# An attention and feed-forward kernel: a fifth tile takes the second product by seven products, and the work around it is laid out again

## The chip, the cores and the metric

The kernel runs on one core of one Trainium2 chip. A core has five engines that run their own streams of instructions and wait for one another by semaphores: TensorE (PE in the profile; PEld is its loading of weights), VectorE (DVE), ScalarE (ACT), GpSimd (POOL) and SyncE (SP, which here issues every transfer). The metric is the device time of one execution in microseconds (us); the figure for a kernel is the median of its runs.

## The reference

Two parts follow each other. The first is a linear attention over 8 batches of 8 heads, with 576 positions and 64 features each; its result is normalised and laid side by side into x, 4608 rows of 512. The second is a feed-forward layer with 2048 inner features.

```python
kv = np.einsum('bhsd,bhse->bhde', k, v)
out = np.einsum('bhsd,bhde->bhse', q, kv)
rms = np.sqrt(np.mean(out * out, axis=-1, keepdims=True) + 1e-06)
attn = out / rms * g_norm
x = attn.transpose(0, 2, 1, 3).reshape(4608, 512)
h = x @ w_in                      # 512 -> 2048
g = h * (1.0 / (1.0 + np.exp(-h)))
return (g @ w_out).astype(np.float32)
```

q, k, v and g_norm are float32; w_in and w_out arrive as float64 and are turned into float32 pairs on the chip.

## The kernel before

**Numbers.** TensorE multiplies in a float32 form with fewer bits. So each operand is kept as an upper part (rounded to that form) and a lower part (what is left, also in that form), and a product is three multiplies: upper by lower, lower by upper, upper by upper. An upper part is made by a copy on ScalarE, a lower part by a subtraction on VectorE or GpSimd. The names `gh`/`gl` are such a pair for the gated values; `wi f` and `wo f` hold both parts of block f (of 16, `NF`) of w_in and w_out.

**Tiles.** The 4608 rows are 9 tiles of 512 (`NT`), run one after the other. A tile goes through 8 steps (`HF`), each of which makes two blocks of 128 inner features (f and f + 8) and gives them to the second product. There are three ways to do that. Tiles 0 and 1 multiply plainly. Tiles 2 to 4 use `pair_step`: the first product of a step, a 2 by 2 product of blocks, is made by seven block products instead of eight (`product`, L782: 7 x 6 = 42 multiplies of 128x256); the second product is plain (`project`, which calls `halves`, L556: 48 multiplies), and runs a step behind. Tiles 5 to 8, set by `OUT7 = 5`, use `seven_step`: here the second product too is made by seven (`multiply`, L958: 42 multiplies), for which sums of the gated values (`first_forms`, `last_form`, `lower_summed`, L917 to L931) and sums of blocks of w_out are needed. The results of a tile of sevens are put together at the end of the tile or within the next one (`copies`, `sums`, `after_switch`). The last tile ends in `seven_end`.

**Order.** The order of the instructions of every engine is that in which the program writes them. Besides the products there are jobs, kept in tables by step g (16 of them in a tile, so 2 in a pair step or a seven step) and by the place in the step (`first_jobs`, `mid_jobs`, `last_jobs`: thirds): the attention of batches 2 to 7 (`plan`), a batch being a block of 80 small multiplies (`mm_kv`, L278) and four groups (`mm_out`, L383) with two transposes, a scaling and a reduction on VectorE for each (L340, L348, L398, L402), with the inverse roots of the batch (L524, L529, L532, L250 to L252); the sums of blocks of w_in (`make_sums`, in tile 1, L636 to L645) and of w_out (`make_out_sums`, in tiles 2 to 4); the sums of x and the operands of the next tile (`sums_of_x`, L726, `make_lower`, L774); and loads. The sums of both weights begin with `whole`, which adds the two parts of a block to the full value (L636 for w_in, L668 for w_out), on VectorE. Sums of w_out go to DRAM as two stores of 512 KB for each j, and come back in tiles 5 to 8 with three or four loads of 256 KB in each step.

**Banks.** PSUM has 8 banks: four accumulate the second product (`acc`), two take the first (`hp`), two are left to attention and, from tile 5 on, to the sevens (`at`, `other`). VectorE adds what the products leave in `hp` (L836 to L864 in pair steps, L1169 to L1215 in sevens) and so frees the bank for the next step's products. In `seven_step` the second product is a queue of 42 multiplies a step that is taken in four windows, `W7 = 12, 11, 11, 8`, between the first product's multiplies.

## Time and profile before

| what | value |
| --- | --- |
| runs | 801.3, 812.69, 812.34 us; median 812.34 |
| profiled execution | span 810.6 us; it has no time of its own beside the span |
| PE busy | 799.9 us, 99% of the span, 7340 instructions |
| DVE busy | 593.1 us, 73%, 1280 instructions |
| ACT busy | 392.9 us, 48%, 817 instructions |
| POOL busy | 112.4 us, 14%, 116 instructions |
| DMA | 171.08 MB; queue 1 takes 61.4% of the sixteen engines' span |

Busy time is the time in which an instruction of the engine ran. Multiplies are pipelined, so a busy TensorE says only that it had work, not at which pace it went. The pace is read from a timeline: two rows that stand at the same place of two steps in a row, their starts, and the multiplies between. Of the windows below, 107.6 to 212 us is tile 1, 212 to 495 the tiles 2, 3 and 4 with the first step of tile 5 (which still finishes tile 4), and 574 to 653 a tile of sevens.

### The profile page before, as it was taken

The page shows a single profiled execution, that of the slowest core. Times are in us where ns is not written, and L with a number is a line of the kernel's source. Part 1 is how long each engine was busy: PE and PEld are TensorE (multiplying, and loading weights), DVE is VectorE, ACT ScalarE, POOL GpSimd, SP SyncE. Part 2 cuts the span into 40 slices and gives each one's busy share as a digit, 9 for nine tenths or more (in the row PEclk, how much of TensorE's full clock was granted, in tenths as well). Part 3 has the DMA queues.
Part 4 walks back from the last instruction along what each step waited for, and adds up shares of the span by engine and source line. Part 5 has one row for each costly group of instructions (what it writes and reads, how often), then busy time and mean ns, then how long its engine had stood idle before and what let it go on. Part 6 is the DMA issues. An engine that isn't in the chain of part 4 may idle for free.

```text
span 810.6 us, 18450 instructions
## 1 busy us (share of the span) xinstructions
PE 799.9 (99%) x7340; PEld 780.3 (96%) x7340; DVE 593.1 (73%) x1280; ACT 392.9 (48%) x817; POOL 112.4 (14%) x116
## 2 busy tenths in 40 slices
PE   8999999999999999999999999999999999999997
PEld 7899999999999999999999999999999999999997
DVE  4999955788667678666767577678867876787666
ACT  4887544434434445435534444336534543464343
POOL 2799771332000000000000000000000000000000
PEclk9999999999999999999999999999999999999999
DMA  9994013645466946866576338876676567657553
GB/s 347 412 410 131 1 60 116 210 164 207 172 217 219 312 150 226 297 230 236 175 253 217 130 131 278 277 242 210 212 246 206 192 203 254 198 183 235 183 182 118
DMA packets 86744, 171.08 MB, mean 211 GB/s; under 512 B 8322, under 2 KB 47746, under 8 KB 86658
## 3 DMA queue, kind: packets, MB, share of 16 engines
q1 hardware_dynamic: 86658, 169.90, 61.4%
q8 instruction: 58, 0.95, 0.5%
q14 instruction: 28, 0.23, 0.1%
HBM read 137.36 MB, written 32.51 MB: 210 GB/s over the span
## 4 chain that ended last, share of the span: by engine, by line
PE 91%; DMA 4%; POOL 2%; issue 1%; DVE 1%; SPq 1%; ACT 0%; DVEq 0%; POOLq 0%; ACTq 0%
PE hp L782 34%; PE acc L556 26%; PE acc L958 11%; PE hp L556 9%; PE at L958 5%; DMA wi<-in_moe_w_in 3%; PE hp L958 3%; PE at L278 2%; PE at L383 2%; DMA k<-in_k 1%; POOL wo L217 1%; SPq L267 0%; POOL gl L577 0%; DVE ob L1009 0%; POOL wo_full L183 0%
## 5 line engine op out<-in xcount | busy, mean ns | idle before, releaser
L556 PE MATMUL acc<-wo,gh 128*128 128x256 f32 x1280 | 201.1, 277 | 0.2 <-POOL wo L217 0.2
L556 PEld LDWEIGHTS acc<-wo,gh 128*128 128x128 f32 x1280 | 170.2, 188 | 4.0 <-issue 3.5
L782 PE MATMUL hp<-x_second,wi 128*128 128x256 f32 x1152 | 156.5, 280 | 0.0
L782 PEld LDWEIGHTS hp<-x_second,wi 128*128 128x128 f32 x1152 | 143.1, 188 | 4.1 <-issue 3.9
L556 PE MATMUL acc<-wo,gl 128*128 128x256 f32 x640 | 124.6, 276 | 0.0
L782 PE MATMUL hp<-operand,wi 128*128 128x256 f32 x912 | 122.8, 279 | 0.3 <-DVE wi L864 0.2
L782 PEld LDWEIGHTS hp<-operand,wi 128*128 128x128 f32 x912 | 113.1, 188 | 0.8 <-DVE wi L864 0.4
L556 PEld LDWEIGHTS acc<-wo,gl 128*128 128x128 f32 x640 | 96.4, 188 | 0.0
L904 ACT ACTIVATE wi<-wi 128x512 f32<-128x512 f32 x64 | 40.5, 632 | 102.3 <-DVE wi L1206 78.0
L1009 POOL TENSOR_TENSOR e<-e,partial 128x256 f32<-128x256 f32 x2 | 1.5, 732 | 606.6 <-DVE e L1009 606.6
L958 PE MATMUL acc<-wo,gh 128*128 128x256 f32 x256 | 48.1, 281 | 0.0
L556 PEld LDWEIGHTS hp<-x_second,wi 128*128 128x128 f32 x384 | 44.8, 188 | 3.1 <-issue 2.6
L556 PE MATMUL hp<-x_second,wi 128*128 128x256 f32 x384 | 47.1, 279 | 0.0
L556 PE MATMUL hp<-x,wi 128*128 128x256 f32 x360 | 44.5, 278 | 0.8 <-POOL x L507 0.8
L958 PE MATMUL acc<-s,gs 128*128 128x256 f32 x288 | 44.1, 281 | 0.0
L556 PEld LDWEIGHTS hp<-x,wi 128*128 128x128 f32 x360 | 42.4, 188 | 1.2 <-POOL x L507 1.0
L1206 DVE TENSOR_TENSOR wi<-hp,partial 128x256 f32<-128x256 f32 x32 | 13.6, 425 | 38.9 <-PE hp L782 38.9
L958 PEld LDWEIGHTS acc<-wo,gh 128*128 128x128 f32 x256 | 39.0, 188 | 0.0
L958 PEld LDWEIGHTS acc<-s,gs 128*128 128x128 f32 x288 | 38.3, 189 | 0.0
L782 PE MATMUL hp<-moved,wi 128*128 128x256 f32 x288 | 37.8, 281 | 0.0
L1191 ACT COPY wi<-hp 128x256 f32<-128x256 f32 x32 | 11.9, 372 | 52.0 <-PE hp L782 52.0
L958 PE MATMUL acc<-wo,gl 128*128 128x256 f32 x128 | 35.9, 281 | 0.0
(213 smaller groups left out, 1559.7 us busy)
## 6 DMA issues: line engine op xcount, KB each, us to landing
wi<-sums_in_dram SPq DMA_DIRECT2D x112, 512.0 KB, 3.5
s<-out_sums SPq DMA_DIRECT2D x96, 256.0 KB, 4.4
wi<-in_moe_w_in SPq DMA_DIRECT2D x16, 512.0 KB, 8.0
wo<-in_moe_w_out SPq DMA_DIRECT2D x16, 512.0 KB, 9.0
sums_in_dram<-sum_parts SPq DMA_DIRECT2D x16, 512.0 KB, 2.9
out_sums<-wi SPq DMA_DIRECT2D x16, 512.0 KB, 2.9
k<-in_k SPq DMA_DIRECT2D x28, 288.0 KB, 5.1
v<-in_v SPq DMA_DIRECT2D x28, 288.0 KB, 5.3
```

The source lines that it names most:

```text
L217: nc.gpsimd.tensor_tensor(out=w[:, 1, :], in0=full, in1=w[:, 0, :].bitcast(F32), op=ALU.subtract)
L278: nc.tensor.matmul(out=self.kv[h], lhsT=self.k[rows, c, :], rhs=self.v[rows, c, :], start=(start and r == 0), stop=(stop and r == 4),)
L383: nc.tensor.matmul(out=self.banks[r][to], lhsT=kv[rows, 2 * self.u + i], rhs=self.q[rows, i * HS:(i + 1) * HS], start=True, stop=True,)
L556: nc.tensor.matmul(out=to[:, at:at + 256], lhsT=stationary, rhs=moving[:, at:at + 256], start=start and at == 0, stop=stop and at == n - 256,)
L782: nc.tensor.matmul(out=out, lhsT=a_of(i, a, c), rhs=x[b][:, c], start=start and n == 0, stop=n == 5, skip_group_check=not check,)
L904: nc.scalar.activation(out=self.gated, in_=self.gated, func=AF.Silu)
L958: nc.tensor.matmul(out=self.out[m], lhsT=g[m], rhs=self.weight(m, j, a), start=j == 0 and n == 0 and m in self.opens, stop=j == HF - 1 and ...
L1009: engine.tensor_tensor(out=to, in0=x, in1=y, op=op)
L1191: nc.scalar.copy(out=first.gated[:, low], in_=u)
L1206: nc.vector.tensor_tensor(out=first.gated[:, high], in0=u, in1=u3, op=ALU.add)
```

## The change

`OUT7` becomes 4: tile 4 too takes the second product by seven, so tiles 2 and 3 alone are pair tiles. What hangs on it is moved. All of attention's multiplies are now done before tile 4 by new tables of thirds (`PLANS`, `QUARTERS`, `SUMS`, `OUT_SUMS`). The adds of `whole` go to GpSimd, all 32 of them. The w_out sums are stored in four parts of 256 KB for each j, straight from the tiles in which they are made. In `seven_step` the operations of the two halves are joined into one where they stood side by side; the queue takes products 1, 2, 3 of both halves and then 5, 7, 6, 4 of both, with `W7 = 11, 12, 11, 8`, and keeps 11 multiplies back from step to step (only the last step of the kernel empties it); the loads of w_out sums stand behind the first window. The first step of tile 4 (`opening`) finishes tile 3's second product by single multiplies, `OPENING = 10, 10, 9, 6`, and 13 more in the next step. Copies, sums and stores of a finished tile of sevens have a table of their own (`between`).

```diff
+QUARTERS = {
+    3: (133, 127, 119, 134),
+    4: (168, 166, 172, 178),
+}
+SUMS = (53, 58, 62, 63, 66, 71, 79, 82)
+OUT_SUMS = (99, 111, 117, 122, 128, 149, 159, 167)
+SUM_STAGES = (2, 4, 1, 1)
+OUT_STAGES = (0, 2, 3, 4, 6, 7)
...
+    OPENING = 10, 10, 9, 6
+    SECOND_AT = 3
     WARM = 2
-    OUT7 = 5
-    AT = {1: 3, 2: 14, 3: 23, 4: 32, 5: 41, 6: 51, 7: 60}
+    OUT7 = 4
...
+    places = const.tile([P, 6, TN], F32R, name="places")
+    gated_kvm = const.tile([P, 2, TN], F32, name="gated_kvm", tag="last_places")
...
+    def gated_place(n):
+        turns[n] += 1
+        return places[:, 3 * n + (turns[n] - 1) % 3]
...
+    def project_calls(t, f, gh, gl, bank, n, cs):
         first, last = order(t)[0], order(t)[-1]
         w = parts["wo", f]
         ns = slice(n * P, (n + 1) * P)
         bank = bank[:, :cs.stop - cs.start]
         terms = ((gh, 1), (gh, 0), (gl, 0)) if t else ((gh, 0), (gl, 0), (gh, 1))
-        for i, (g, a) in enumerate(terms):
-            halves(bank, g[:, ns], w[:, a, cs], f == first and i == 0, f == last and i == 2)
-        if f == last and t + 1 == OUT7:
-            emptied.append(lambda: empty(t, bank, n, cs, True))
-        elif f == last:
-            empty(t, bank, n, cs, n % 2)
+        columns = range(0, cs.stop - cs.start, 256)
+        def multiply(i, g, a, c):
+            nc.tensor.matmul(
+                out=bank[:, c:c + 256], lhsT=g[:, ns], rhs=w[:, a, cs][:, c:c + 256],
+                start=f == first and i == 0 and c == 0, stop=f == last and i == 2 and c == columns[-1],
+            )
+        def end():
+            if f == last and t + 1 == OUT7:
+                emptied.append(lambda: empty(t, bank, n, cs, True))
+            elif f == last:
+                empty(t, bank, n, cs, n % 2)
+        calls = [lambda i=i, g=g, a=a, c=c: multiply(i, g, a, c) for i, (g, a) in enumerate(terms) for c in columns]
+        return calls[:-1] + [lambda: (calls[-1](), end())]
+    def project(*item):
+        for call in project_calls(*item):
+            call()
...
+    def whole(engine, to, kind, f):
+        w = parts[kind, f].bitcast(F32)
+        engine.tensor_tensor(out=to, in0=w[:, 0, :], in1=w[:, 1, :], op=ALU.add)
...
-            lambda: whole(lower, i),
-            lambda: whole(upper, i + HF),
+            lambda: whole(nc.gpsimd, lower, "wi", i),
+            lambda: whole(nc.gpsimd, upper, "wi", i + HF),
...
-        def upper(two):
-            nc.scalar.copy(out=both_parts[:, 0], in_=two)
+        def upper(half, two):
+            nc.scalar.copy(out=uppers[:, half], in_=two)
         def lower(half, two):
-            nc.vector.tensor_tensor(out=both_parts[:, 1], in0=two, in1=both_parts[:, 0].bitcast(F32), op=ALU.subtract)
-            nc.sync.dma_start(out=out_sums[j, half], in_=both_parts.bitcast(F32))
+            nc.vector.tensor_tensor(out=two, in0=two, in1=uppers[:, half].bitcast(F32), op=ALU.subtract)
+            for part, w in enumerate((uppers[:, half].bitcast(F32), two)):
+                nc.sync.dma_start(out=out_sums[j, half][:, part], in_=w)
+        def first_three():
+            combine(s41[:, high], s41[:, high], s23[:, high], ALU.add)
+            combine(s23[:, high], s23[:, low], s23[:, high])
+            combine(s23[:, low], s41[:, high], s23[:, low])
+        def wholes():
+            whole(nc.gpsimd, s23, "wo", j)
+            whole(nc.gpsimd, s41, "wo", j + HF)
+        def fourth():
+            combine(s41[:, low], s41[:, low], s23[:, low])
+            upper(0, s23)
         return [
-            lambda: whole(s23, j),
-            lambda: whole(s41, j + HF),
-            lambda: combine(s41[:, high], s41[:, high], s23[:, high], ALU.add),
-            lambda: combine(s23[:, high], s23[:, low], s23[:, high]),
-            lambda: combine(s23[:, low], s41[:, high], s23[:, low]),
-            lambda: upper(s23),
-            lambda: combine(s41[:, low], s41[:, low], s23[:, low]),
+            wholes, first_three, fourth,
+            lambda: upper(1, s41),
             lambda: lower(0, s23),
-            lambda: None,
-            lambda: None,
-            lambda: None,
-            lambda: upper(s41),
-            lambda: None,
...
+    def both_lower_plain():
+        y = once["both_gated"]
+        nc.vector.tensor_tensor(
+            out=plain[1][:, :, :3 * P], in0=y[:, :, P:], in1=plain[0][:, :, :3 * P].bitcast(F32), op=ALU.subtract
+        )
+    def both_forms():
+        y, f = (once[name].rearrange("p h (k n) -> p h k n", n=P) for name in ("both_gated", "forms"))
+        nc.vector.tensor_tensor(
+            out=f[:, :, 0:2], in0=y[:, :, 1:3], in1=y[:, :, 0:1].to_broadcast([P, 2, 2, P]), op=ALU.subtract
+        )
+        nc.vector.tensor_tensor(out=f[:, :, 2], in0=y[:, :, 2], in1=f[:, :, 0], op=ALU.add)
+        nc.vector.tensor_tensor(out=f[:, :, 3], in0=y[:, :, 3], in1=f[:, :, 2], op=ALU.subtract)
+    def both_upper_summed():
+        nc.scalar.copy(out=summed[0], in_=once["forms"])
+    def both_lower_summed():
+        nc.vector.tensor_tensor(
+            out=summed[1], in0=once["forms"], in1=summed[0].bitcast(F32), op=ALU.subtract
+        )
     class Half:
...
-    W7 = 12, 11, 11, 8
+    W7 = 11, 12, 11, 8
...
-            (0, "I"): [c[0], *made_ahead(3)], (0, "II"): [c[1], c[2], a[0], a[1]], (0, "III"): a[2:4],
-            (1, ""): [lambda: nc.scalar.copy(out=fourths, in_=once["fourths"])],
-            (1, "I"): [d[0], d[1], *a[4:6]], (1, "II"): [d[2], a[6], b[0], b[1]], (1, "III"): b[2:4],
-            (2, "I"): b[4:6], (2, "II"): b[6:],
+            (0, ""): [*under(5), *uppers(3)], (0, "I"): under(3), (0, "II"): [c[0]],
+            (1, ""): [c[1], d[0], a[0]],
+            (1, "II"): [c[2], d[1], lambda: nc.scalar.copy(out=fourths, in_=once["fourths"]), d[2], a[1], a[2]],
+            (1, "III"): a[3:5], (2, ""): a[5:7], (2, "II"): [*b[0:2], a[7]], (2, "III"): [*b[2:4], a[8]],
+            (3, ""): b[4:6], (3, "II"): [b[6], b[7]], (3, "III"): b[8:],
         })
...
-            queue.extend(item for half in sevens for item in half.items(j, half.order))
+            for ms in (1, 2, 3), (5, 7, 6, 4):
+                queue.extend(item for half in sevens for item in half.items(j, ms))
         def window(n):
-            if opening:
-                for item in groups[:2]:
-                    project(*item)
-                del groups[:2]
+            if opening or ((t, i) == (OUT7, 1) and n == 0):
+                count = OPENING[n] if opening else len(groups)
+                for call in groups[:count]:
+                    call()
+                del groups[:count]
                 return
-            count = len(queue) if n == 3 else (W7 if later else (11, 10, 10))[n]
+            count = len(queue) if last and n == 3 else W7[n]
             for half, *item in queue[:count]:
...
-        load_out_sums(i, 5, 7, 6)
         begin(g)
         product(1, i, u, True, False)
         product(6, i, v, False, False)
         if not opening:
-            first.upper_summed()
-            second.upper_plain()
-            second.first_forms()
-            second.last_form()
-            first.lower_summed()
+            both_forms()
         nc.scalar.copy(out=p1, in_=u)
...
-        window(0)
+        if (t, i) != (OUT7, 1):
+            window(0)
+        load_out_sums(i, 5, 7, 6)
         if not opening:
-            second.lower_plain()
-            second.upper_summed()
-            second.lower_summed()
+            both_upper_summed()
...
+        if not opening:
+            both_lower_summed()
...
-        nc.vector.tensor_tensor(out=first.gated[:, high], in0=u, in1=u3, op=ALU.add)
-        nc.vector.tensor_tensor(out=second.gated[:, high], in0=v, in1=u3, op=ALU.add)
+        nc.vector.tensor_tensor(
+            out=once["both_gated"][:, :, high], in0=bank.rearrange("p (h n) -> p h n", n=H),
+            in1=u3.unsqueeze(1).to_broadcast([P, 2, H]), op=ALU.add,
+        )
         slot("III")
         first.gate()
         first.upper_plain()
-        first.first_forms()
+        if last:
+            first.first_forms()
         window(2)
         run(mid_jobs.pop(g + 1, ()))
         product(3, i, v, False, False)
         nc.vector.tensor_tensor(out=second.gated[:, low], in0=v, in1=u2, op=ALU.add)
         second.gate()
-        first.last_form()
-        first.lower_plain()
...
+        for n, (p, f) in enumerate(zip(ps, jobs)):
+            at_third(loads[n], lambda p=p: p.load(which="kv"))
+            at_third(q_loads[n], f.load)
+            at_third(jobs_at[n], lambda f=f: f.mm_out(kv[0]), f.copy_out)
+            at_third(turns[n], f.turn_sq)
+            at_third(sums_at[n], *[begin] * (n == 0), lambda f=f: f.sum_turned(norms[0]))
+            at_third(roots[n], lambda n=n: some((6, 3, 3, 3)[n]))
+            for part in (0, 1) if b == 2 else (None,):
+                at_third(scales[n], lambda p=p, part=part: p.spread(norms[1][:, p.c], part))
+                at_third(scales[n] + (b > 2), lambda p=p, part=part: p.scale(part))
+            at_third(keeps[n], p.keep)
+        at_third(kv_at, kv_block)
+        at_third(copy_at, copy_kv)
+        return ps
...
-        for j, g in enumerate((33, 37, 41, 49, 53, 57, 65, 69)):
-            spread_out(lambda j=j: make_out_sums(j), 3 * g, *[1] * 14)
+                at_third(QUARTERS[t][n], lambda t=t, n=n: load_quarter(t, n))
+        for j in range(HF):
+            calls = []
+            def some(j, calls=calls):
+                if not calls:
+                    calls.extend(make_out_sums(j))
+                calls.pop(0)()
+            for n in range(6):
...
```

Counted over the program, TensorE has 48 multiplies of 128x256 fewer (6885 to 6837) and all others as before; VectorE has 191 instructions fewer, ScalarE 18 fewer, GpSimd 32 more, and the transfer queue 42 more.

On TensorE, within tile 4, the order before has the plain second product (L556, `acc`) between the products of the first (L782, `hp`); `gh` and `gl` are the gated values.

```order
L556 MATMUL acc<-wo_583,gh 128x256 x4
L556 MATMUL acc<-wo_583,gl 128x256 x2
L782 MATMUL hp<-operand_3017,wi_564 128x256 x6
L782 MATMUL hp<-operand_3056,wi_3013 128x256 x6
L556 MATMUL acc<-wo_1408,gh 128x256 x4
L556 MATMUL acc<-wo_1408,gl 128x256 x2
```

The changed program has in the same tile, with `places` and `summed` in the place of `gh`, `gl` and `gs`, and `s` the sums of w_out (L889 is the first product, L1076 the second):

```order
L889 MATMUL hp<-x_second,wi_1134 128x256 x6
L889 MATMUL hp<-x_second,wi_2924 128x256 x6
L1076 MATMUL acc<-wo_1293,places 128x256 x3
L1076 MATMUL acc<-wo_574,places 128x256 x3
L1076 MATMUL at<-s,places 128x256 x2
L1076 MATMUL at<-s,summed 128x256
L1076 MATMUL hp<-s,places 128x256 x2
```

The second product of tile 4 now reads sums and writes the banks of attention (`at`, `hp`) as well.

On VectorE, a block of w_out sums in a pair tile before: `s_5668` and `s_5669` are the tiles in which the sums are made, L668 the adds of the two parts.

```order
L668 TENSOR_TENSOR s_5668<-wo_1059 128x512
L855 TENSOR_TENSOR gf<-hp,wi_3153 128x256
L856 TENSOR_TENSOR gf<-hp,wi_3153 128x256
L598 COPY wi_3249<-acc 128x512
L398 STREAM_TRANSPOSE sqT<-sq 128x576
L668 TENSOR_TENSOR s_5669<-wo_1774 128x512
L864 TENSOR_TENSOR wi_3153<-hp,wi_3153 128x256
L796 TENSOR_TENSOR gl<-gf,gh 128x512
```

In the changed program the two adds of such a block stand on GpSimd (L738), one behind the other:

```order
L738 TENSOR_TENSOR s_3834<-wo_765 128x512
L738 TENSOR_TENSOR s_3835<-wo_1439 128x512
```

and VectorE begins the block with the combinations (L774), the first of which waits for GpSimd:

```order
L774 TENSOR_TENSOR s_3835<-s_3835,s_3834 128x256 [waits Pool_49]
L774 TENSOR_TENSOR s_3834<-s_3834 128x256 [waits DVE_49]
L774 TENSOR_TENSOR s_3834<-s_3835,s_3834 128x256 [waits DVE_49]
L968 TENSOR_TENSOR wi_3084<-hp,wi_3084 128x256 [waits PE_49]
L903 TENSOR_TENSOR places<-gated_kvm,places 128x512 [waits Activation_49]
```

What frees a bank (L968, L864 before) stands behind the combinations and so behind GpSimd's adds.

On VectorE, the last pair step of tile 2 in the changed program, which makes the operands of the next tile (L881) and the sums of x (L833) beside attention's squares (L491, L495):

```order
L941 TENSOR_TENSOR wi_3084<-hp,wi_3084 128x256
L903 TENSOR_TENSOR places<-wi_3084,places 128x512
L833 TENSOR_TENSOR t_4149<-x_1_2037,t_4148 128x512
L491 STREAM_TRANSPOSE sqT<-sq 128x576
L951 TENSOR_TENSOR wi_3084<-hp,wi_3084 128x256
L881 TENSOR_TENSOR operand_2926<-x_0_1871,operand_2926 128x512
L881 TENSOR_TENSOR operand_2965<-t_4148,operand_2965 128x512
L495 TENSOR_REDUCE sums<-sqT 128x2x9
L960 TENSOR_TENSOR wi_3084<-hp,wi_3084 128x256
L961 TENSOR_TENSOR wi_3084<-hp,wi_3084 128x256
```

Before, that step held such operands with one transpose for attention; now it holds two transposes and two reductions.

## Rows read from the trace of the kernel before

**Rows 1.** The page: busy time, the granted clock in tenths, the chain.

```profile
PE 799.9 (99%) x7340; PEld 780.3 (96%) x7340; DVE 593.1 (73%) x1280; ACT 392.9 (48%) x817; POOL 112.4 (14%) x116
...
PEclk9999999999999999999999999999999999999999
...
PE 91%; DMA 4%; POOL 2%; issue 1%; DVE 1%; SPq 1%; ACT 0%; DVEq 0%; POOLq 0%; ACTq 0%
```

**Rows 2.** Windows: stretch, length; PE, PEld, DVE, ACT, POOL busy; clock, DMA.

```profile
107.60:212.00 104.40, 104.40 (x1036) 100.05 (x1037) 71.75 (x133) 45.39 (x97) 31.19 (x25) 1.00 0.47 168
212.00:495.00 283.00, 282.75 (x2718) 271.68 (x2717) 200.39 (x434) 125.78 (x267) 0.00 (x0) 1.00 0.63 211
574.00:653.00 79.00, 79.00 (x673) 79.00 (x673) 59.56 (x145) 38.79 (x78) 0.00 (x0) 1.00 0.66 213
```

**Rows 3.** Timeline of PE in tile 4: start, length, instruction.

```profile
472.89 1.52 PE L782 MATMUL hp<-operand,wi 128*128 128x256 f32 x12
...
483.09 1.52 PE L782 MATMUL hp<-operand,wi 128*128 128x256 f32 x12
```

**Rows 4.** The same view in tiles 5, 6 and 8.

```profile
503.12 1.73 PE L782 MATMUL hp<-operand,wi 128*128 128x256 f32 x12
...
592.32 1.58 PE L782 MATMUL hp<-moved,wi 128*128 128x256 f32 x12
...
602.21 1.58 PE L782 MATMUL hp<-moved,wi 128*128 128x256 f32 x12
...
795.48 1.56 PE L782 MATMUL hp<-moved,wi 128*128 128x256 f32 x12
...
801.00 0.40 PE L958 MATMUL hp<-s,gh 128*128 128x256 f32 x2
801.47 0.38 PE L958 MATMUL hp<-s,gl 128*128 128x256 f32 x1
```

**Rows 5.** The same view where attention stands in tile 2.

```profile
228.87 2.70 PE L278 MATMUL at<-v,k 128*64 128x64 f32 x80
...
251.80 0.39 PE L556 MATMUL acc<-wo,gl 128*128 128x256 f32 x2
252.12 0.72 PE L383 MATMUL at<-q,kv_all 64*64 64x288 f32 x8
252.77 1.64 PE L782 MATMUL hp<-x_second,wi 128*128 128x256 f32 x12
```

**Rows 6.** Groups on DVE, 215 to 495 us: busy, mean ns, idle before.

```profile
L796 DVE TENSOR_TENSOR gl<-wi,gh 128x512 fp32r<-128x512 f32 x24 | 16.4, 682 | 0.0
...
L348 DVE SCALAR_TENSOR_TENSOR o<-o,gcol,yT 128x576 f32<-128x576 f32 x18 | 14.6, 811 | 0.0
L340 DVE STREAM_TRANSPOSE yT<-y 128x576 f32<-128x576 f32 x18 | 13.9, 770 | 0.0
L398 DVE STREAM_TRANSPOSE sqT<-sq 128x576 f32<-128x576 f32 x18 | 13.8, 765 | 0.0
L402 DVE TENSOR_REDUCE sums<-sqT 128x18 f32<-128x576 f32 x18 | 13.4, 744 | 0.0
L668 DVE TENSOR_TENSOR s<-wo 128x512 f32<-128x512 f32 x16 | 10.8, 677 | 0.0
...
L836 DVE TENSOR_TENSOR wi<-hp,wi 128x256 f32<-128x256 f32 x24 | 10.2, 425 | 25.0 <-ACT wi L835 11.9 <-ACT kv_all L1297 7.2 <-PE hp L782 5.3
```

**Rows 7.** What PE waited for from 56 us on: total, times, longest.

```profile
PE hp L782 <- DVE wi L864: 0.2, 1, 0.2
```

**Rows 8.** Groups on POOL, and on DVE in 107 to 212 us.

```profile
L645 POOL TENSOR_TENSOR sum_parts<-sums,sum_parts 128x512 fp32r<-128x512 f32 x16 | 21.4, 1346 | 60.1 <-ACT sum_parts L644 60.1
...
L577 DVE TENSOR_TENSOR gl<-gf,gh 128x512 fp32r<-128x512 f32 x16 | 12.7, 792 | 26.5 <-ACT gf L576 23.5 <-issue 3.0
```

**Rows 9.** Timelines of POOL and DVE in tile 1.

```profile
179.48 2.54 POOL L645 TENSOR_TENSOR sum_parts<-sums,sum_parts 128x512 fp32r<-128x512 f32 x2 [6.84 <-ACT sum_parts L644]
...
180.94 1.64 DVE L577 TENSOR_TENSOR gl<-gf,gh 128x512 fp32r<-128x512 f32 x1 [1.90 <-ACT gf L576]
```

More of the change, by code (lines that the diff above doesn't have):

```diff
@@ L996, in sums @@
                 lambda: add(two[:, high], three[:, low], two[:, high], ALU.subtract),
-                upper_rows, lower_rows,
+                lambda: add(two[:, low], two[:, low], one[:, low]),
+                lambda: add(one[:, low], fourth(), three[:, low]),
+                lambda: self.store(t, 0, slice(0, DM), two),
+                store_lower,
             ]
@@ L1120, in seven_step @@
             open_sevens()
-        if (t, i) == (OUT7, 1):
-            first_banks()
-        first, second = sevens
+        last = (t, i) == (NT - 1, HF - 1)
+        if not opening:
+            first, second = sevens
         if t + 1 < NT and i == 5:
@@ L1173, in seven_step @@
             open_gated()
+            first, second = sevens
         while lowers:
@@ L1176, in seven_step @@
             make_lower(m, home(m))
+        if (t, i) == (OUT7, 1):
+            window(0)
+            second.upper_plain()
+        if not opening:
+            both_lower_plain()
         slot("")
@@ L1192, in seven_step @@
         nc.vector.tensor_tensor(out=u3, in0=v, in1=p1, op=ALU.add)
+        if not opening:
+            both_lower_summed()
         if later:
@@ L1216, in seven_step @@
         second.gate()
-        first.last_form()
-        first.lower_plain()
+        if last:
+            first.last_form()
+            first.lower_plain()
+        elif not opening:
+            second.upper_plain()
         if later:
@@ L1317, in plan, with some @@
-        for p in ps if b == 1 else ():
+        kv = []
+        loads, (kv_at, copy_at), q_loads, jobs_at, turns, sums_at, roots, scales, keeps = PLANS[b]
+        jobs = [Job(b, n, ps[n // 2 * 2:n // 2 * 2 + 2]) for n in range(NP)]
+        calls = []
+        def some(count):
+            if not calls:
+                calls.extend(rsqrt(*norms, False))
+            for _ in range(count):
+                calls.pop(0)()
[10 more added lines that the diff above has]
+            at_third(keeps[n], p.keep)
```

255 lines of the change are left out of this document (133 added, 122 removed).

## The prediction, as it was made before the changed kernel ran

> **What bounds the kernel now.** I read the page first: TensorE is busy for 99% of the span, VectorE for 73%, and 91% of the chain that ends last is TensorE [rows 1]. The reader is to see that no other engine or transfer sets the end over a longer stretch. The windows by tile say the same of each stage: from 107.6 us on TensorE is busy for the whole of each stretch, VectorE for 71% of the pair tiles and 75% of a tile of sevens, and the granted clock is 1.00, which is the 2.4 GHz level [rows 2]. The waits confirm it: from 56 us on only one wait is booked, 0.2 us for VectorE's L864 [rows 7]. So the time is the number of multiplies times their pace, and the next thing to read is the pace.
>
> In tile 4 two equal places of neighbouring steps lie 10.20 us apart (472.89 to 483.09) with 90 multiplies of 128x256 between: 113.3 ns each [rows 3]. In tile 6 the distance is 9.89 us (592.32 to 602.21) for 84: 117.8 ns [rows 4]. The pace changes at one place: the row at 503.12, the start of tile 5's third step, has twelve multiplies in 1.73 us where the row at 472.89 has 1.52; from there to about 796 us a row of twelve has 1.58, and at 795.48 it is on its way back to 1.52 [rows 3, 4]. The granted clock reads 1.00 on both sides. These 293 us hold about 29.6 steps of 84; at 4.44 ns each that is 11.05 us. The lowest run is 801.3, and 812.3 - 11.05 = 801.3. I take it that the profiled execution and the two runs at 812 have that stretch, and that the lowest run has not. What starts it the rows don't tell.
>
> The profiled execution has only its span, 810.6 us; the median of the runs is 812.34, 1.7 above. I make the sum against the span and add 1.7.
>
> **The change part by part.**
>
> *Fewer multiplies.* Tile 4 has 8 steps of 42 + 42 multiplies in place of 42 + 48: 48 fewer, none of another kind added. At 113.3 ns: 48 x 0.1133 = **-5.44 us**, all of it on the path, since TensorE is the path.
>
> *Pace of tile 4.* If the slower pace belongs to the sevens, it now begins a tile earlier: 8 x 84 x 4.44 ns = **+2.98 us**. If it doesn't, 0. It has its start in the sevens in the one execution that there is, so I take 2.98 and keep 0 as a rival.
>
> *Joined operations of the sevens.* VectorE does 59.56 us in a tile's 79 [rows 2], and no multiply of the sevens waits for it [rows 7]. Joining saves starts of instructions where nobody waits: 0. The queue's new order and the 11 multiplies held back give the next step's sums more time, and the loads of w_out sums behind the first window are used a step, some 9.9 us, later. Also 0. At the end of the kernel multiplies stand still for some tenths: the pair at 801.00 should be followed 0.24 later, and the next row starts at 801.47, 0.23 too late [rows 4]. There now stand 19 multiplies behind the last product where 11 stood, about 0.9 us more cover, for this and a second such gap: **-0.5**, bounds 0 and -0.5.
>
> *Opening and hand-over.* Tile 3's second product is finished by single multiplies in the opening and 13 in the second step: the same multiplies at the same pace, in another order. Result copies and stores go by another table; those of a tile of sevens lie beside multiplies, under VectorE's free quarter. 0, with 1 us either way for a bank that comes free late.
>
> *Transfers.* 32 stores of 256 KB in the place of 16 of 512, and 24 more loads of 256 KB (tile 4's) pass SP's queue, which is busy for 0.63 to 0.66 in these tiles [rows 2]. What hides them is the step between load and use. If that cover went, a load would cost its own time once, which the bound of 1 us above includes.
>
> *Pair tiles with more VectorE work each.* This is the part with a real price. Attention of six batches, the operands and all of the w_out sums must now be done before tile 4. In the 283 us of tiles 2 to 4 VectorE has 200.39 us of work [rows 2]. Of that go the own work of 8 steps (five operations like L836 at 0.425 and two like L796 at 0.682, 3.49 us a step, 27.9), and the sixteen adds of L668 (16 x 0.677 = 10.8) [rows 6]. Two of 18 attention groups (L348, L340, L398, L402: 3.09 us each, 6.2) stand in tile 1 now. That leaves about 156 us. TensorE in tiles 2 and 3 has 16 x 10.20 = 163.2, 16 groups of attention at about 0.86 (0.97 from 251.80 to 252.77, less two multiplies of 0.113, and 0.12 by which the twelve behind it are longer, 1.64 for 1.52) and three blocks of keys and values at some 2.6: about 185 [rows 3, 5]. So VectorE goes from 71% to 84%. Priced step by step with those rows, one step of sixteen has more work for VectorE than for TensorE: the last of tile 2, with five operations at 0.425, nine at 0.683, two transposes at 0.770 and two reductions at 0.744, 11.3 us, against 90 x 0.1133 + 0.86 = 11.1. Steps 4, 5 and 6 of that tile have some 0.8, 1.0 and 0.5 us to spare. The one wait of before, at L864, is such a step [rows 7].
>
> *GpSimd's adds.* An add of 128x512 on GpSimd takes 1.346 us (L645), on VectorE 0.677 [rows 6, 8]. GpSimd has nothing to do in the pair tiles (0.00 [rows 2]), so its own length costs nothing, but VectorE's first combination waits for the pair, and L864's successor, which frees TensorE's bank, stands behind that. And a running add lengthens what VectorE does beside it: the sixteen L577 have a mean of 0.792 where the like of L796 has 0.682, and one that began under two adds took 1.64 and ended at 182.58, 0.56 after the second add's end at 182.02 [rows 6, 8, 9]. It stood still for most of the add. Sixteen L577 lost 16 x 0.11 = 1.76 us, and in the timeline four of them are longer than 0.69: 0.44 each. Sixteen adds that each meet one such operation: 7 us, 0.9 for each of the eight blocks of sums, and a block's step has 0.5 to 4 us to spare. The excess is some tenths in two or three steps, with the full step of 11.3 beside them: **+1.0** in all. Bounds: 0, and 5.7 more under the rivals. In tile 1 the same happens under VectorE's 71.75 of 104.4 us [rows 2]: 0.
>
> The Trainium skill (SBUF — State Buffer, section "SBUF: two separate sides") has a rule that speaks against this part: VectorE with two inputs in SBUF and GpSimd share a port pair as a lock, and the one that comes second stands until the other's whole instruction is done. The row at 180.94 agrees with it; by the rule the adds would cost what the third rival below has, by the mean of L577 the 1.0 of the sum.
>
> **Sum.** -5.44 + 2.98 - 0.5 + 1.0 = -1.96; span 810.6 to 808.6, and with 1.7 for the median: **810.3 us**.
>
> **The rivals.** *First, the slower pace doesn't grow:* it starts by something else than the sevens, and lasts as long as before. For it: at 1.00 both stretches have the same granted clock. Against: it began two steps into the sevens, and the lowest run seems to lack all of it. Time: 810.3 - 2.98 = 807.4.
>
> *Second, no slower pace in the runs that make the median:* as the lowest run of before has it. 801.3 - 5.44 - 0.5 + 1.0 = 796.4. One of three runs speaks for it, two and the profiled one against.
>
> *Third, GpSimd's adds hold VectorE, and VectorE TensorE:* the place is the combination behind the two adds in the pair tiles. Two adds in a row take 2.54 us [rows 9]; if VectorE stands for both, a block costs 2.54 less what its step has to spare. With 1.0, 4.4, 0.8, 1.0, 0.5 in tile 2 and 2.7 or more in tile 3 (reckoned as above) that is 1.5 + 0 + 1.7 + 1.5 + 2.0 + 0 = 6.7, in place of the 1.0: 816.0, slower than before. It decides from 3.0 us on (5.44 - 2.98 + 0.5). For it: the long L577. Against: the adds of L577's stretch lengthened few of its operations, and five of the seven own operations of a step have an input in PSUM, as L836.
>
> *That the change does not do what it says* is excluded as far as the multiplies go: the 48 are gone from TensorE's order.
>
> **Chances.** Forecast 0.45; first rival 0.20, second 0.20, third 0.10; anything else (a late operand, a bank that comes free late, a load) 0.05. The range reaches from the second rival less 1 us of the unpriced parts to the third: 795.4 to 816.0. About 2% is what a measurement of this kernel can tell from no change; that is below 796.1 or above 828.6. Faster by more takes the lower half of the second rival: 0.10. Slower by more needs three times the third rival's price: 0.03. Same: 0.87.
>
> **What would show it.** In the profile after: 6837 multiplies of that kind; twelve multiplies in 1.52 in tiles 2 and 3 and 1.58 from tile 4's third step on (1.52 there: the first rival; 1.52 everywhere: the second). VectorE at about 84% of tiles 2 and 3; waits of TensorE for L968 there of some tenths, about 1 us in all (7: the third, with VectorE idle behind POOL, or operations such as L903 above 1 us). At the end no gap before the last sums. The forecast is wrong if tiles 2 and 3 take over 3 us more than their multiplies, or if the pace is another one.

## The result: slower by 1.4%, and the profile after

| | median | lowest to highest | runs |
| --- | --- | --- | --- |
| before | 802.24 us | 800.38 to 813.25 | 20 |
| changed | 814.61 us | 806.88 to 820.02 | 20 |

The changed kernel takes 1.0136 times as long, 95% interval [1.0108, 1.0164]. The time lies inside the range of the forecast and on its other side: 12.4 us longer instead of 2 shorter. The 812 us that stood as the median of before was that of three runs; of twenty, fifteen are at 800 to 803 and five at 812 to 813. So the slower pace, which the forecast took for the usual case, is before's exception.

The page of the changed kernel, profiled at a span of 808.9 us: busy time, the chain by line, one group of adds on GpSimd (mean 1514 ns), and the landing of two kinds of load.

```profile
span 808.9 us, 18271 instructions
...
PE 791.7 (98%) x7292; PEld 769.3 (95%) x7292; DVE 595.5 (74%) x1089; ACT 406.3 (50%) x799; POOL 158.5 (20%) x148
...
PE 60%; DMA 4%; DVE 4%; issue 0%; POOL 0%; DVEq 0%; SPq 0%; POOLq 0%
...
L738 POOL TENSOR_TENSOR s<-wo 128x512 f32<-128x512 f32 x16 | 24.1, 1514 | 136.8 <-DVE sqT L491 53.7
...
wi<-sums_in_dram SPq DMA_DIRECT2D x112, 512.0 KB, 4.4
s<-out_sums SPq DMA_DIRECT2D x120, 256.0 KB, 3.9
```

Against [rows 1], TensorE is idle for 17.2 us of the span (808.9 - 791.7) instead of 10.7. The chain is followed over 68% of the span only, so its 60% can't be set against 91%; but VectorE has 4% of it where it had 1%. The w_in sums land in 4.4 us where they took 3.5; the page of before has:

```profile
wi<-sums_in_dram SPq DMA_DIRECT2D x112, 512.0 KB, 3.5
```

What TensorE waited for in the changed kernel from 56 us on: total, times, longest. It answers to [rows 7].

```profile
PE hp L889 <- DMA wi<-sums_in_dram: 3.3, 3, 2.1
PE hp L889 <- DVE wi L941: 1.8, 1, 1.8
PE acc L703 <- DVE places L669: 0.5, 1, 0.5
PE hp L889 <- DVE partial L1285: 0.3, 1, 0.3
PE hp L889 <- DVE wi L1331: 0.2, 1, 0.2
PE hp L889 <- DVE wi L951: 0.2, 1, 0.2
PE hp L889 <- DVE wi L968: 0.2, 1, 0.2
```

The view leaves out what a pipelined engine loses around a wait. So for every profile I took the starts of the 128x256 multiplies from 56 us on. A distance over 121 ns counts as a standstill with what it has above 113.3 (the first one behind a group of attention is 221 or so in each profile without a wait, and counts with what it has above that); one of 115.5 to 121 counts as a multiply at the slower pace, with 4.44 ns.

| profile | span | standstills | slower pace | rest |
| --- | --- | --- | --- | --- |
| before | 810.6 | 1.9 | 11.4 | 797.3 |
| changed | 808.9 | 12.1 | 4.3 | 792.5 |

The rest fell by 4.8, near the 5.44 of the 48 multiplies. Standstills rose by 10.1, and that is more than the gain. Without any slower pace the changed kernel's row would give 792.5 + 12.1 and some 1.8 us from span to time, 806.4; the lowest of its twenty runs has 806.88. So most of its runs seem to have more of the slower pace than the profiled one; that is an estimate, since only one run has a trace.

The windows of the changed kernel (columns as in [rows 2]): tiles 2 and 3, tile 4, a tile of sevens.

```profile
212.00:408.00 196.00, 193.73 (x1917) 182.26 (x1916) 156.50 (x315) 92.53 (x203) 24.09 (x16) 1.00 0.72 235
408.00:497.00 89.00, 86.33 (x750) 85.36 (x750) 63.81 (x116) 42.43 (x77) 0.00 (x0) 1.00 0.76 245
...
576.00:654.00 78.00, 77.86 (x679) 77.62 (x678) 55.44 (x98) 40.11 (x71) 0.00 (x0) 1.00 0.68 216
```

TensorE stands still for 2.3 us in tiles 2 and 3 and 2.7 in the stretch of tile 4; VectorE's share is 80% in the first (the forecast had 84%), with GpSimd 24 us beside it. The two places with the largest waits show two different causes.

GpSimd and VectorE at the end of tile 1 and the beginning of tile 2, from the changed kernel's timelines (start, length, instruction):

```profile
215.78 1.29 POOL L738 TENSOR_TENSOR s<-wo 128x512 f32<-128x512 f32 x1 [14.35 <-DVE sums L495]
219.31 1.65 POOL L738 TENSOR_TENSOR s<-wo 128x512 f32<-128x512 f32 x1 [2.24 <-DVE x_second L881]
...
215.65 1.88 DVE L617 COPY m<-sums 32x72 f32<-32x72 f32 x4
...
219.75 1.75 DVE L881 TENSOR_TENSOR x_second<-x,x_second 128x512 fp32r<-128x512 f32 x1
221.43 0.41 DVE L941 TENSOR_TENSOR wi<-hp,wi 128x256 f32<-128x256 f32 x1
```

L881 takes 0.68 elsewhere in this stretch and 1.75 under the add of 219.31; four copies take 1.88 under the first add, where the like take 0.80 at 411. That is 2.1 us, and L941 behind them, which frees the bank, is 1.8 us late. GpSimd runs its adds as soon as a buffer is free (it waited 14.35 us for it), not where the program has them beside other work. Before the wait at 186 us it is the same: an operation of L345 that takes 0.23 elsewhere takes 1.23 at 181.34, and one of L441 that takes 0.42 at 187.51 takes 1.29 at 184.16, under the adds at 181.17 and 183.91:

```profile
181.17 1.31 POOL L738 TENSOR_TENSOR lower<-wi 128x512 f32<-128x512 f32 x1
...
181.34 1.23 DVE L345 SCALAR_TENSOR_TENSOR y<-u,y 128x72 f32<-128x72 f32 x1
```

L343 and L344 just ahead take 1.32 and 1.22, under the lower parts (L752) that GpSimd makes in both kernels. The Trainium skill (SBUF — State Buffer, "SBUF: two separate sides") has this as a lock on a port pair that is held for the whole instruction; the rows agree with it, also for operations as small as 0.23 us.

SyncE's queue and TensorE in the second and third step of tile 4, changed kernel:

```profile
417.07 0.53 SPq L1154 DMA_DIRECT2D wo<-out_sums  x1
420.79 0.34 SPq L691 DMA_DIRECT2D out<-ob  x1
421.17 2.57 SPq L1154 DMA_DIRECT2D s<-out_sums  x3
...
424.48 0.38 SPq L818 DMA_DIRECT2D wi<-sums_in_dram  x1
...
430.76 0.97 PE L889 MATMUL hp<-operand,wi 128*128 128x256 f32 x6 [2.09 <-DMA wi<-sums_in_dram]
```

Three loads of w_out sums (768 KB) and stores go out just ahead of the load of w_in sums at 424.48, which TensorE needs 4.2 us later (the multiplies of 427.82 end at 428.6); it lands in some 6 us. The w_out sums themselves are not used for another step.

### The profile page after: what moved, and what is told of

Read it like the earlier page. It is cut to its first block, busy times and chain, and to the rows that moved or that the text cites. A ratio compares the mean times of both kernels' runs of the same rounds, so it can differ in the third digit from the quotient of the medians.

```text
span 808.9 us, 18271 instructions
## 1 busy us (share of the span) xinstructions
PE 791.7 (98%) x7292; PEld 769.3 (95%) x7292; DVE 595.5 (74%) x1089; ACT 406.3 (50%) x799; POOL 158.5 (20%) x148
## 4 chain that ended last, share of the span: by engine, by line
PE 60%; DMA 4%; DVE 4%; issue 0%; POOL 0%; DVEq 0%; SPq 0%; POOLq 0%
PE hp L889 29%; PE acc L1076 13%; PE acc L703 7%; PE at L1076 6%; DMA wi<-sums_in_dram 3%; PE hp L1076 3%; PE at L476 1%; DVE s L774 1%; PE at L371 1%; DMA out_sums<-s 1%; DVE places L903 0%; DVE s L780 0%; DVE ob L1125 0%; DVE x_second L881 0%; DVE m L617 0%
## 5 line engine op out<-in xcount | busy, mean ns | idle before, releaser
L703 PE MATMUL acc<-wo,places 128*128 128x256 f32 x1536 | 192.8, 277 | 0.7 <-DVE places L669 0.5
L703 PEld LDWEIGHTS acc<-wo,places 128*128 128x128 f32 x1536 | 182.4, 188 | 3.9 <-issue 2.6
L889 PE MATMUL hp<-x_second,wi 128*128 128x256 f32 x1152 | 155.2, 279 | 2.8 <-DVE wi L941 1.8
L889 PEld LDWEIGHTS hp<-x_second,wi 128*128 128x128 f32 x1152 | 141.4, 188 | 8.4 <-issue 2.6
L889 PE MATMUL hp<-operand,wi 128*128 128x256 f32 x864 | 116.2, 279 | 2.5 <-DMA wi<-sums_in_dram 2.1
L1022 ACT ACTIVATE wi<-wi 128x512 f32<-128x512 f32 x80 | 50.6, 632 | 125.5 <-DVE wi L1331 108.2
L889 PEld LDWEIGHTS hp<-operand,wi 128*128 128x128 f32 x864 | 106.2, 188 | 5.3 <-DMA wi<-sums_in_dram 2.3
L1076 PE MATMUL acc<-wo,places 128*128 128x256 f32 x520 | 85.3, 277 | 0.0
L1076 PEld LDWEIGHTS acc<-wo,places 128*128 128x128 f32 x520 | 71.2, 188 | 0.0
L738 POOL TENSOR_TENSOR s<-wo 128x512 f32<-128x512 f32 x16 | 24.1, 1514 | 136.8 <-DVE sqT L491 53.7
L1000 ACT CAST places<-wi 128x1024 fp32r<-128x1024 f32 x39 | 41.2, 1057 | 18.9 <-PE acc L1076 18.9
L1076 PE MATMUL acc<-s,places 128*128 128x256 f32 x240 | 49.2, 277 | 0.0
L1076 PE MATMUL at<-wo,places 128*128 128x256 f32 x360 | 47.6, 277 | 0.0
L1003 DVE TENSOR_TENSOR summed<-wi,places 128x1024 fp32r<-128x1024 f32 x39 | 47.4, 1216 | 0.0
L993 DVE TENSOR_TENSOR wi<-wi 128x512 f32<-128x512 f32 x39 | 27.0, 693 | 26.6 <-ACT wi L1022 26.6
L889 PE MATMUL hp<-moved,wi 128*128 128x256 f32 x336 | 44.0, 278 | 0.9 <-DMA wi<-sums_in_dram 0.9
L1076 PEld LDWEIGHTS at<-wo,places 128*128 128x128 f32 x360 | 44.1, 188 | 0.0
```

The lines of the kernel that those rows point to most:

```text
L703: nc.tensor.matmul(out=bank[:, c:c + 256], lhsT=g[:, ns], rhs=w[:, a, cs][:, c:c + 256], start=f == first and i == 0 and c == 0, stop=f == ...
L738: engine.tensor_tensor(out=to, in0=w[:, 0, :], in1=w[:, 1, :], op=ALU.add)
L889: nc.tensor.matmul(out=out, lhsT=a_of(i, a, c), rhs=x[b][:, c], start=start and n == 0, stop=n == 5, skip_group_check=not check,)
L993: nc.vector.tensor_tensor(out=f[:, :, 0:2], in0=y[:, :, 1:3], in1=y[:, :, 0:1].to_broadcast([P, 2, 2, P]), op=ALU.subtract)
L1000: nc.scalar.copy(out=summed[0], in_=once["forms"])
L1003: nc.vector.tensor_tensor(out=summed[1], in0=once["forms"], in1=summed[0].bitcast(F32), op=ALU.subtract)
```

## Experiments

**e1.** All 32 adds back on VectorE: `whole(nc.gpsimd, ...)` becomes `whole(nc.vector, ...)` in four places.

> The changed kernel with all 32 adds of w's two parts back on VectorE, and nothing else. Theory A (GpSimd's adds hold VectorE): the wait of 2.0 us at 220 us for L941 and the 0.7 at 186 us go (below 0.3 together), since no copy or lower part there is lengthened any more; waits for VectorE between 260 and 310 us (about 1.3 us) shrink or stay; the waits for w_in sums (3.3 us, a transfer) stay; with the same pace of the multiplies the span is 2 to 3 us shorter. Theory B (VectorE has too much work in tiles 2 and 3): 16 x 0.68 = 11 us more of VectorE there, waits for VectorE in 215 to 320 us rise from about 3.5 to 6 us or more, and the span is as long or longer.

Measured: median 812.94 (810.45 to 817.3, 4 runs), ratio to before 1.0104 [1.0013, 1.0195]; span 808.3, standstills 13.1. Waits of TensorE, and one of VectorE:

```profile
PE hp L889 <- DVE wi L960: 3.1, 1, 3.1
PE hp L889 <- DMA wi<-sums_in_dram: 2.8, 2, 2.3
PE hp L889 <- DVE gated_kvm L960: 0.7, 1, 0.7
...
DVE s L738 <- DMA out_sums<-s: 4.8, 1, 4.8
```

The waits at 186 and 220 us are gone, as theory A had it, and those for w_in sums stay. But the span is no shorter: VectorE now has the adds in its own stream, and one stood for 4.8 us until a store from the buffer that it writes had landed. That was in neither theory. On GpSimd the same wait holds nobody; the store straight from the buffer and the move to GpSimd belong together. TensorE's wait of 3.1 us (258 us) follows that standstill of VectorE, and behind it the clock was lower for a while (last section), some 1.6 of the 13.1 us. No other booked wait for VectorE is longer than 0.7 us, so work that fills VectorE (theory B) was not the cause.

**e2.** The loads of w_out sums behind that of w_in sums; adds as in the change.

```diff
             window(0)
-        load_out_sums(i, 5, 7, 6)
...
         if later:
             load_sums(i + 1, 0)
+        load_out_sums(i, 5, 7, 6)
```

> The changed kernel with the loads of w_out sums (m 5, 7, 6) issued behind the load of the next step's first half of w_in sums instead of ahead of it; adds stay on GpSimd. Theory C (three loads of 256 KB just ahead of a 512 KB load that is needed 6 us later make it late): the waits of 2.1 us at 429, 0.9 at 517 and 0.3 elsewhere for w_in sums go, below 0.5 in all, and the median landing of w_in sums falls from 4.4 to about 3.5 us; VectorE's waits (about 5 us) stay; with the same pace 2.5 to 3.3 us shorter. Rival D (the queue is late because of result stores and their waits): the waits for w_in sums stay at 2 us or more.

Measured: median 802.93 (801.14 to 815.77, 10 runs), ratio 1.0022 [1.0011, 1.0032]; span 801.2. All waits of TensorE from 56 us on:

```profile
PE hp L889 <- DVE wi L941: 1.5, 1, 1.5
PE acc L703 <- DVE places L669: 0.9, 1, 0.9
PE hp L889 <- DVE partial L1285: 0.3, 1, 0.3
PE hp L889 <- DVE wi L1331: 0.2, 1, 0.2
PE hp L889 <- DVE wi L951: 0.2, 1, 0.2
PE hp L889 <- DVE wi L968: 0.2, 1, 0.2
```

No wait for a transfer is left, and the landing is 3.7 us. Theory C holds, rival D falls: the result stores stayed where they were. Standstills fall from 12.1 to 7.0. Yet the median falls by 11.7 (against before, run beside each, from 12.4 us longer to 1.7), where the expectation had 2.5 to 3.3: from 427 us on this profile has no standstill, and no slower pace either.

**e3.** Both edits.

> Both edits: adds on VectorE, and the loads behind. Theories A and C together: PE waits 5 to 6 us less than in the changed kernel, few waits in tiles 4 to 8, so that the pace of the multiplies stays at 113.3 ns in most runs: median about 800 to 803, no slower than the kernel before. Theory B: 806 or more.

Measured: median 802.76 (801.54 to 818.99, 10 runs), ratio 1.0002 [0.9968, 1.0037]; span 800.9, standstills 8.7. The median is where it was expected, the sum is not: e1's wait for the store is there again (3.5 us at 257), so all adds on VectorE are no better than all on GpSimd.

**e4.** The kernel before, with six added waits.

```diff
         product(3, i, v, False, False)
+        if t > OUT7 and i in (2, 5):
+            for _ in range(3):
+                nc.vector.tensor_scalar(out=once["forms"][:, 0], in0=once["forms"][:, 0], scalar1=1.0, ...)
         nc.vector.tensor_tensor(out=second.gated[:, low], in0=v, in1=u2, op=ALU.add)
```

> The kernel before with one added wait of TensorE of about 1 us at six places: in steps 2 and 5 of tiles 6, 7 and 8 VectorE multiplies a buffer by 1.0 three times (0.69 us each) ahead of the operation that frees the bank. Theory F (the pace of 113.3 or 117.8 ns is drawn anew wherever TensorE stands still for a moment, and kept until the next such place): in the profile the pace changes at one or more of these six places, and nowhere else in tiles 6 to 8 but at a gap; runs spread between about 806 and 815. Theory G (the slower pace belongs to the sevens or to something outside): the pace doesn't change at these places, and each run is that of the kernel before plus the six waits, some 5 us.

Measured: median 808.31 (808.08 to 808.62, 10 runs), ratio 1.0091 [1.0081, 1.0101]. The six waits came (5.5 us in all), of the same length each, and the pace behind all six is 113.3. Theory F as put falls: a standstill does not always change the pace. Theory G is not shown by it either, for none of the ten runs lies some 11 us above the others, as a quarter of before's do.

**e5.** The loads behind, and the adds of w_in and of the first block of w_out on VectorE, the other seven blocks on GpSimd: `nc.gpsimd if j else nc.vector`.

> The loads behind, as in e2, and the adds on VectorE for w_in (tile 1) and for the first block of w_out sums (the one that runs at 215 to 221 us); the other seven blocks stay on GpSimd. Theory A: with no GpSimd add in those two places no small operation of VectorE there takes 1.2 us for 0.23, the waits at 186 us (1.1) and 220 us (1.8) fall below 0.4 together, and the waits at 273 to 299 and 410 to 426 us stay as in e2: span and median 2 to 3 us below e2 (802.9), about 800.3, below the kernel before. Rival H (VectorE is simply full at the end of tile 1): VectorE's own adds take the place, the waits stay at 2 us or more.

Measured: six of twelve runs at 796.5 to 798.3 and six at 811.8 to 812.8, median 805.04; ratio of the first six to before 0.9933 [0.9886, 0.998]. The profile (span 810.0) has 2.8 us of standstills; the waits at 186 and 220 us are gone, so theory A holds and H falls. It also has 15.6 us of slower pace, 14.5 of it behind one standstill of some 0.4 us at 420.5. Its two groups of runs are some 14 us apart, which is what that pace costs; the expected 800.3 lies between them.

**e6.** As e5, and `OUT_SUMS = (99, 111, 117, 128, 149, 159, 167, 174)`.

> As e5, and the blocks of w_out sums begin at thirds 99, 111, 117, 128, 149, 159, 167, 174 in the place of 99, 111, 117, 122, 128, 149, 159, 167: one block less in the crowded steps 5 and 6 of tile 2, one more in step 14, which had 8 us of VectorE for 10.2 of TensorE. Theory A with the load theory: waits of 1.5 us at 273 to 299 us fall below 0.8; median about 799.5. If the moved block meets the stores it waits for, a new wait at 370 to 400 us takes it back: 800 to 801.

Measured: median **796.48** (795.8 to 810.72, 12 runs), ratio to before **0.9934 [0.9905, 0.9963]**. Span 794.9, standstills 1.4, slower pace 1.3; the waits at 270 to 299 us are gone. It beats both kernels, by 18 and by 5 us, and has the change's 48 multiplies less.

**e7.** The kernel before, with the load of the first half of w_in sums in tile 6 behind products 4 and 5.

> The kernel before, with the load of the first half of the next step's w_in sums in tile 6 alone issued behind products 4 and 5 (some 2.6 us later). Theory F2 (the pace of 113.3 or 117.8 ns changes where TensorE waits for a transfer, whose end falls at any moment, and holds until the next such place): TensorE waits up to 1 us for w_in sums in some of the eight steps, the pace changes at some of these places, runs spread from 803 to 815 and their median is more above the kernel before than the waits in the profile add up to. Theory G (pace is independent of waits): runs are the kernel before's plus the waits, with the same share of runs at 812.

Measured: median 801.86 (800.29 to 812.55, 10 runs), ratio 1.0012 [0.9954, 1.0069]. No wait came of it, since the sums landed in 3.4 us and were in time, so it tells nothing of the pace. Of the transfer it tells that 2.6 us less lead are no harm in that tile, where no other loads stand just ahead.

**e8.** e5 with three multiplies by 1.0, as in e4, in step 4 of tiles 4, 5 and 6.

> The kernel of e5 with an added wait of TensorE of about 1 us in step 4 of tiles 4, 5 and 6, made as in e4. In e5 half of the runs are at 797 and half at 812, and the profiled one of the slow half took its slower pace at a wait at 420 us and kept it to the end. Theory F3 (the pace is set at a standstill and kept to the next one): the added standstills, the first some 35 us behind 420, end what was taken there, so that the two groups of runs are no longer 797 and 812: none keeps the slower pace from 420 us to the end, and if the added ones come out as in e4, every run lies between 799 and 804. Theory G (a run has the slower pace for another reason): half of the runs lie near 800.5 and half near 815.5.

Measured: median 799.31 (796.94 to 814.05, 11 runs; six below 800, five above 811), ratio 0.9955 [0.9945, 0.9966]. The added operations took 0.42 us each and were covered, no wait came, and the kernel behaves as e5. The question stayed open.

**e9.** e6 with one reduction and the roots of batch 7 later: in `PLANS[7]`, `(183, 185, 189, 191)` becomes `(183, 185, 189, 193)` and `(193, 194, 195, 196)` becomes `(194, 195, 196, 197)`.

> The kernel of e6 with the last reduction of batch 7 and its roots one or two thirds later, out of the crowded hand-over to tile 4. Load theory: the waits of 0.4 us at 404 and 0.25 at 407 us shrink to under 0.3 together; median 0 to 0.6 us below e6 (796.5), and fewer runs above 800 than e6's 3 of 12, since fewer standstills stand in front of the sevens. Rival: the roots' copies meet the next step's operations instead; the same time as e6.

Measured: median 810.78 (810.15 to 811.42, 6 runs), ratio 1.01 [1.0053, 1.0148]: wrong for both. Standstills are 1.6 us against e6's 1.4. The difference of 14 us is the pace. The windows of both (stretch, length, TensorE busy, multiplies, granted clock, DMA share, GB/s), first e9:

```profile
422.00:800.00 378.00, 378.00 (x3212) 1.00 0.64 216
```

and e6:

```profile
422.00:785.00 363.00, 363.00 (x3205) 1.00 0.67 225
```

378.0/3212 is 117.7 ns, 363.0/3205 is 113.3, both with the clock at 1.00 (2.4 GHz) and without a gap. It is not the chip: e8, which ran beside e9, has six of eleven runs below 800. The pace parts at the standstill at 420 us. TensorE's timeline of e9 there:

```profile
416.94 1.52 PE L889 MATMUL hp<-x_second,wi 128*128 128x256 f32 x12
419.91 0.97 PE L889 MATMUL hp<-x_second,wi 128*128 128x256 f32 x6 [0.20 <-DVE wi L1331]
421.66 1.58 PE L889 MATMUL hp<-operand,wi 128*128 128x256 f32 x12
```

and of e6:

```profile
417.26 1.58 PE L889 MATMUL hp<-x_second,wi 128*128 128x256 f32 x12
420.09 0.97 PE L889 MATMUL hp<-x_second,wi 128*128 128x256 f32 x6
421.81 1.52 PE L889 MATMUL hp<-operand,wi 128*128 128x256 f32 x12
```

In e9 twelve multiplies go from 1.52 to 1.58 there and keep it to the end; in e6 the same place takes them from 1.58, which began at 411, back to 1.52.

**e10 and e11.** e9 with six or eight multiplies by 1.0 in step 4 of tile 4 alone, so that TensorE stands still at 451 us.

> The kernel of e9, whose six runs all lie at 810 to 811 us with the slower pace of 117.8 ns from a standstill at 419 us to the end, with one added standstill: in step 4 of tile 4 VectorE multiplies a buffer by 1.0 six times (0.42 us each) ahead of the operation that frees the bank, so that TensorE waits some 0.5 to 1.5 us at about 455 us. Theory F3 (the pace is set at a standstill and kept to the next one): the slower pace ends or is drawn anew there. If it comes out at 113.3, the run becomes shorter by 13 us less the wait, about 797 to 800, although work was added; if at 117.8, it is 811 to 812 as before. Theory G (the slower pace has nothing to do with standstills): 811 to 812 in every run, and no change of pace at 455.

> As e10 with eight multiplies in place of six, so a standstill about 0.85 us longer. Theory F3: the pace behind it depends on how the standstill ends, so it can be the other one than in e10; it is one of the two in every step behind it. Theory G: e10's time plus 0.85.

Measured: e10 798.52 (798.36 to 799.1, 3 runs), ratio 0.9897 [0.9776, 1.0018]; e11 799.91 to 813.76 in 9 runs, four at 800 to 802 and five at 812 to 814, ratio 1.0048 [0.9984, 1.0113]. With one wait of 0.93 us added, e10 is 12 us shorter than e9. But its profile has the usual pace again already at 420, ahead of the added wait, so it doesn't show the added wait doing it. In that of e11 the slower pace ends at the added wait:

```profile
422.28 1.58 PE L889 MATMUL hp<-operand,wi 128*128 128x256 f32 x12
...
447.61 1.58 PE L889 MATMUL hp<-x_second,wi 128*128 128x256 f32 x12
...
453.86 2.35 PE L889 MATMUL hp<-operand,wi 128*128 128x256 f32 x11 [1.74 <-DVE wi L1348]
...
458.20 0.84 PE L889 MATMUL hp<-operand,wi 128*128 128x256 f32 x6
```

Twelve in 1.58 up to the wait, six in 0.84 (0.87 at the slower pace) behind it, and no slower pace again to the end of that run. The clock fell for some us behind the same wait (last section), so this place alone doesn't tell whether the standstill or the fall ended the slower pace; at 420 us the clock stayed at 1.00. Theory F3 holds for what these profiles show; G falls. In all thirteen profiles, before's and the changed kernel's among them, no stretch between two distances over 121 ns (40 to 58 stretches in each) holds a change of pace. In seven of them the slower pace is taken at 420 us or later, and each time it stays to the next such place or to the end of the multiplies. Which of the two comes out is not settled: the standstill at 420 us ended in the slower one in e9's profile and, by their times, in all of its runs, and in half of e5's; e9, e10 and e11 are the same program up to there.

The traces show more of that place. In e6, e8 and e10 TensorE arrives at the slower pace, the distance is 236 to 238 ns, and it leaves at 113.3; in e5, e9 and e11 it arrives at 113.3, the distance is 476 or 477, and it leaves at the slower pace. Rows ahead of and behind the place, first e10, then e5:

```profile
417.52 1.58 PE L889 MATMUL hp<-x_second,wi 128*128 128x256 f32 x12
...
422.07 1.52 PE L889 MATMUL hp<-operand,wi 128*128 128x256 f32 x12
```

```profile
418.01 1.52 PE L889 MATMUL hp<-x_second,wi 128*128 128x256 f32 x12
...
422.74 1.58 PE L889 MATMUL hp<-operand,wi 128*128 128x256 f32 x12
```

So the moment of arrival goes with the outcome there. It is no rule: e2 and e3 have 511 and 478 at the same place of their order, and 113.3 on both sides.

## Why the prediction was wrong, point by point

*The pace.* The step "if the slower pace belongs to the sevens" failed, and with it the base of the sum: the 812.34 and the 810.6 of before hold some 11 us of a slower pace that most of its runs don't have. The pace is taken at a standstill and kept (e9, e11); the sevens only have nothing that would end it, while attention's groups in tiles 1 to 3 do: up to 408 us no slower stretch of the thirteen profiles is longer than 82 multiplies, and in before's tiles 5 to 8 one has 2474. In before it was taken at 503.69, where two distances of 190 and 226 ns stand in the row of 1.73 [rows 4]; by the trace the multiply at 503.88 was released by the landing, at 503.83, of the load of w_in sums that was issued at 497.87. The second rival, with a fifth of the chance, had before's usual run right. Its 796.4 is near e6's 796.48, which has the fewer multiplies and hardly a wait.

*The 48 multiplies.* -5.44 is borne out: the rest of the table fell by 4.8 in the changed kernel, and e6 is 5.2 below before.

*Transfers.* "What hides them is the step between load and use", 0 with 1 us at most, was asked of the moved loads only. They had a step to spare; the load behind them in the queue had about 4 to 6 us, and became late. I counted who uses the moved loads and not what stands behind them in the same queue. It cost 5.1 us of standstills (e2), and with it undone the median falls by 11.7. The other 6.6 I put down to the pace; that is argued and not shown, since of each kernel one run has a profile and the others only a time. In the profiled runs the pace is 2.9 of the 7.7.

*GpSimd's adds.* The mechanism was named, its price put at 1.0, and the third rival had 6.7. Measured: 7.0 us of standstills are left in e2, 1.9 in before; about 3 of them at 186 and 220 us go with the adds of those places (e5), 1.4 with one block moved (e6). So the 1.0 was too small, and the rival's price was near with its place wrong. Of the two largest of these waits one (186 us) is in tile 1's last 35 us, put at 0 by VectorE's mean share of the tile; the other (220 us) is in tile 2's first step, where operations that ran under the adds made L941 late. The pair's first combination, the rival's named place, waited once for 0.5 us.

*Joined operations, hand-over, end.* Joining and end are right as far as seen: VectorE's share in a tile of sevens fell from 75% to 71%, and no gap stands before the last sums. The hand-over costs 1.8 us of standstills from 409 to 427 us in the changed kernel (0.5 of them booked as waits for VectorE), where the forecast had 0 with 1 us either way; in e6 they are 1.3 of the 1.4 us left.

*The range* held the time by luck: the upper end was the third rival's, with before's slower pace in the base; what came was new waits and more of the slower pace than before's usual run has, a case that the forecast did not have.

## What to carry to other kernels

On an in-order queue, price a moved transfer by what now stands behind it: how soon each later one is needed and how many bytes go ahead of it. A mean share of an engine hides the end of a stage; lay the moved operations beside the last operations before the stage's first product. Where one engine is busy all the time, take the median of before from enough runs, and look at the pace of equal pieces of work in each profile before comparing spans.

## What was not expected of the hardware

Two steady paces of the same multiplies, 113.3 and 117.7 ns, at the same granted clock of 1.00, with no gap in either for 360 us and more; the change from one to the other comes at a standstill, of some tenths of a us in e9 and of 2 us in e11, and what decides it is open. After e11's standstill of 2 us the granted clock fell as well, to 0.51, the 1.2 GHz level, for 3.2 us with most of 17 multiplies 213 ns apart (windows: stretch, length, TensorE busy, granted clock, DMA share, GB/s):

```profile
451.90:454.60 2.70, 0.96 (x7) 0.95 0.95 328
454.60:457.80 3.20, 3.20 (x17) 0.51 0.26 92
457.80:470.00 12.20, 12.20 (x110) 1.00 0.57 195
```

The clock fell likewise behind the standstills of 3.3 and 3.5 us at 258 and 257 us: to 0.51 from 262.0 to 265.4 in e1, and to 0.53 from 261.6 to 265.2 in e3. Behind the changed kernel's waits of 1.8 us at 220 and 2.1 at 429 it stayed at 1.00.
